# A second first-stage table, reads back in 4 KB pieces, and staging tiles in other buffers

## The chip, the core and the metric

The kernel runs on one core of one Trainium2 chip. The metric is device time in microseconds (us) of one execution. Before the change the median of 3 runs is 520.27 us (519.3 to 520.41).

## What is computed

Two blocks stand behind each other. The first filters each of 8 sequences (2496 tokens, 256 channels) in the frequency domain; the second sends every token to one of 8 experts, of which each keeps the 80 tokens with the largest gate, and all other rows of the output are zero.

```python
X = np.fft.rfft(x, axis=1); Y = X * (filt_r + 1j * filt_i)[None]
y = np.fft.irfft(Y, n=2496, axis=1).reshape(8 * 2496, 256)
logits = y @ w_gate; expert_idx = np.argmax(logits, axis=1)
gate_w = softmax(logits)[arange(N), expert_idx]
for e in range(8):
    tok = the (at most capacity = 80) tokens of expert e with the largest gate_w
    out[tok] = gate_w[tok, None] * (np.maximum(y[tok] @ w1[e], 0) @ w2[e])
```

## The kernel before, in words

All matmuls are in float32. The transform of 2496 = 39 x 64 points is done in two stages. For every batch b (0 to 7), the first stage (`stage1`, 11 parts k, each of two groups i of three columns) multiplies an x chunk, 117 partitions of 3 x 39 rows, with the table `wf_t` (117 x 120: NJ = 3 columns, 2 for real and imaginary, NS = 20 frequencies). It does that in one of two ways.

- `still` (L331 to L336), for batches 0, 3, 4, 5 and 7: x is the stationary side, in two halves of 128 channels, and `wf_t` moves, through a rearranged view: the table lies as (a s), with a = (real or imaginary, column), and is read as (s a), 20 elements apart. The result lies channel by channel, is copied to `t1` by ScalarE (L377, VectorE for part of batch 0), and `transpose1` (L420, L422) turns it with identity matmuls into `t2` tiles.
- `moving` (L338 to L341), for the batches in `BOUNCE` = (1, 2, 6): `wf_t` is the stationary side and x moves, 256 columns. ScalarE copies the result to a staging tile `sg` (L347, L348, from `t2pool`, 4 tiles that the `t2` of `transpose1` share), stores it to DRAM (L352, 1 KB pieces), and `take` (L407 to L413) reads it back transposed from DRAM: three DMAs for a batch, of partitions 0-48, 48-96 and 96-128, each a row of 20 KB per partition. There are no transposes for these batches.

The second stage (`stage2`, 10 steps u for a batch, so v = 10 b + u from 0 to 79) multiplies with `d_t` (L432), VectorE multiplies the result with the filter (two L440), POOL adds and subtracts (L447). Two steps later `turn` multiplies with the identity and the gate weights at once (L460); ScalarE copies the spectrum out (L476) to `ys` (batches 0 and 1) or `ysp` tiles of `fspool` (3 tiles of 4 KB a partition), which go to DRAM (L453). Logits, gates and each batch's candidates follow from there. After the 80 steps come the choice of the kept tokens, their inverse transform from the spectra read back (L588, L609) and the experts (L1278, L1293).

The order is written out by hand (`manual_schedule`): in step v come stage2(v), `take`, the x loads that are due (`put_x`, with a table `held` of the earliest steps), the transposes of step v + 2, the stage1 parts that `s1_at` lists for v, some zero stores of the output (L202), then turn(v - 2). SP's queue carries, in program order, the x loads, the `d_t` loads, the zero stores and the reads back; ScalarE's queue carries the stores; POOL's the filter loads (L285) and other gathers. The PSUM pool `fps` has 3 banks, which L333, L339, L420 and L432 use in turn. A one-element copy `mark` on POOL (L954) holds the later filter loads until an x chunk has come.

Of the kernel before, what the change touches and what calls it, by code (L numbers as in the profile page):

```python
# [13 lines left out]
F32 = mybir.dt.float32  # L14
BF16 = mybir.dt.bfloat16
I32 = mybir.dt.int32
# [7 lines left out]
B, S, C = 8, 2496, 256  # L24
N = B * S
N1, N2 = 39, 64
NS, NQ = 20, 64
NU = NS // 2

NJ, NG = 3, 21  # L30
# [3 lines left out]
SG = 4  # L34
NP, NA = B // 2, N1 + 1
SP = 32
E, FF = 8, 1024
# [4 lines left out]
def dft_tables():  # L42
    n1, n2 = np.arange(N1), np.arange(N2)
    s, q = np.arange(NS), np.arange(NQ)
    ph = 2 * np.pi * (np.outer(n1, s) % N1) / N1
    w = np.stack([np.cos(ph), -np.sin(ph)], 1)
    wf = np.zeros((N1, NJ, 2, NJ, NS))
    for j in range(NJ):
        wf[:, j, :, j] = w

    k = np.array([[next(m for m in range(i, S, N1) if m % NQ == j) for j in q] for i in s])
    th = 2 * np.pi * (n2[:, None, None] * k % S) / S
    c, sn = np.cos(th), np.sin(th)
    d = np.zeros((2, N2, NS, 2, NQ))
    d[0, :, :, 0], d[1, :, :, 0] = c, sn
    d[0, :, :, 1], d[1, :, :, 1] = -sn, c

    two = np.where(s == 0, 1.0, 2.0) / S
    be = 2 * np.pi * (np.outer(q, n2) % NQ) / NQ
    back = np.zeros((2, NQ, 2, N2))  # L60
    back[0, :, 0], back[1, :, 0] = np.cos(be), -np.sin(be)
    back[0, :, 1], back[1, :, 1] = np.sin(be), np.cos(be)
    wi = np.zeros((4, SP, 2, N1, 4))
    for e in range(4):
        wi[e, :NS, 0, :, e] = (two * np.cos(ph)).T
        wi[e, :NS, 1, :, e] = (-two * np.sin(ph)).T

    n = (39 * n2[:, None] + 64 * n1) % S
    al = 2 * np.pi * (n.reshape(S, 1, 1) * k % S) / S
    rows = np.stack([np.cos(al), -np.sin(al)], 2) * two[:, None, None]  # L70

    frow = np.minimum(k, S - k).reshape(NU, 128).T
    fsig = np.where(k > S // 2, -1.0, 1.0).reshape(NU, 128).T
    f32 = np.float32

    def places(a):
        g = a[:, :NJ * NG].reshape(2, NJ, NG, NS, -1).transpose(2, 0, 1, 3, 4)
        return np.concatenate([g.reshape(NJ * 2 * NG, NS, -1), a[:, -1].reshape(2, NS, -1)])

    return (wf.reshape(NJ * N1, -1).astype(f32), wi.reshape(4 * SP, 2, 4 * N1).astype(f32),  # L80
            places(d).reshape(128, NS, 128).astype(f32), back.reshape(128, 128).astype(f32),
            rows.reshape(S, NS * 128).astype(f32),
            np.ascontiguousarray(frow).astype(np.int32), np.ascontiguousarray(fsig).astype(f32))
# [3 lines left out]
def kernel(  # L87
# [11 lines left out]
    nc = tc.nc  # L99
# [17 lines left out]
    dpool = ctx.enter_context(tc.tile_pool(name="dram", bufs=1, space=DRAM))  # L117

    cand = consts.tile([128, B, KC], F32, name="cand")
    warm = cand[:].rearrange("p b k -> p (b k)").bitcast(BF16)  # L120
    nc.vector.memset(warm, 0.0)
    ident = consts.tile([128, 128], F32, name="ident")
# [33 lines left out]
    for b in range(B):  # L156
# [9 lines left out]
    nc.vector.tensor_scalar(out=thot[:], in0=iota[:, 0:16], scalar1=trow[:, 0:1], scalar2=None,  # L166
                            op0=AL.is_equal)
    ehot_t = consts.tile([E, 128], F32, name="ehot_t")
    ecol_i = consts.tile([128, 128], I32, name="ecol_i")
    nc.vector.tensor_single_scalar(out=ecol_i[:], in_=iota_i[:], scalar=E - 1,  # L170
                                   op=AL.bitwise_and)
    ecol = consts.tile([128, 128], F32, name="ecol")
    nc.vector.tensor_copy(out=ecol[:], in_=ecol_i[:])
    nc.vector.tensor_scalar(out=ehot_t[:], in0=ecol[0:E], scalar1=pid[0:E, 0:1], scalar2=None,
                            op0=AL.is_equal)
    same = consts.tile([128, 128], BF16, name="same")
    nc.vector.tensor_scalar(out=same[:], in0=ecol[:], scalar1=lane[:, 0:1], scalar2=None,
                            op0=AL.is_equal)
    before = consts.tile([128, 128], BF16, name="before")
    nc.vector.tensor_scalar(out=before[:], in0=iota[:], scalar1=pid[:, 0:1], scalar2=None,  # L180
# [60 lines left out]

    zs = [consts.tile([128, 2, E, SP], F32, name=f"z_{i}") for i in range(2)]
    key = consts.tile([128, 48, E], F32, name="key")
    kt = consts.tile([128, 2, N2, 4], F32, name="kt")

    with ExitStack() as actx:
        bctx = ExitStack()
# [18 lines left out]

        NM = NJ * 2 * NS
        t_dram, takes = {}, []
        wf_t = tpool.tile([NJ * N1, NM], F32, name="wf_t")
        d_t = tpool.tile([128, NS, 128], F32, name="d_t")  # L270
        e_t = lpool.tile([128, 2 * N2], F32, name="e_t")
# [53 lines left out]
        def stage1(b, k):  # L325
            xt = st["x", b, 2 * k // JC]
            full = 2 if k < NB - 1 else 1
            nk = 2 if full == 2 or b % NJ == 0 else 1
            trio = [i for i in range(B) if min(i - i % NJ, B - NJ) == min(b, B - NJ)]

            def still(ps, i):  # L331
                for cb in range(NDB):
                    nc.tensor.matmul(  # L333
                        out=ps[:, i, NM * cb:NM * cb + NM],
                        lhsT=xt[0:NJ * N1, (2 * k + i) % JC, 128 * cb:128 * cb + 128],
                        rhs=wf_t[:].rearrange("p (a s) -> p s a", s=NS), start=True, stop=True)  # L336

            def moving(ps, i):  # L338
                nc.tensor.matmul(  # L339
                    out=ps[0:NM, i], lhsT=wf_t[:],  # L340
                    rhs=xt[0:NJ * N1, (2 * k + i) % JC, :], start=True, stop=True)  # L341

            if b in BOUNCE:
                ps = fps.tile([128, 2, C], F32, name=f"pa_{b}_{k}", tag="f")
                for i in range(nk):
                    moving(ps, i)
                sg = t2pool.tile([128, 2, C], F32, name=f"sg_{b}_{k}", tag="t2")  # L347
                nc.scalar.copy(out=sg[0:NM, 0:nk], in_=ps[0:NM, 0:nk])  # L348
                if k == 0:
                    t_dram[b] = dpool.tile([128, NS, C], F32, name=f"t_{b}")  # L350
                p0 = 2 * NJ * 2 * k
                nc.scalar.dma_start(  # L352
                    out=t_dram[b][p0:p0 + 2 * NJ * full].rearrange("(i a) s c -> (a s) i c", i=full),
                    in_=sg[0:NM, 0:full])
                if nk > full and b % NJ == 0:
                    left = [i for i in trio if i not in BOUNCE]
                    put_last(b, sg[:, 1])
                    if left:
                        assert len([i for i in trio if i in BOUNCE]) == 1
                        ps = fps.tile([128, 2, NDB * NM], F32, name=f"pm_{b}", tag="f")  # L360
                        still(ps, 1)
                        keep_left(left[0], ps[:, 1], 128)
                elif k == NB - 1:
                    put_last(b, st["left"])
                if k in (3, 7, NB - 1):
                    takes.append((b, k))
                return

            if k == 0:
                st["t1", b] = t1pool.tile([128, NDB * NS, 128], F32, name=f"t1_{b}", tag="t1")  # L370
            t1 = st["t1", b]
            ps = fps.tile([128, 2, NDB * NM], F32, name=f"pa_{b}_{k}", tag="f")
            for i in range(nk):
                still(ps, i)
            copy = nc.vector.tensor_copy if b == 0 and k % 3 == 1 else nc.scalar.copy
            p0 = 2 * NJ * 2 * k
            copy(out=t1[:, :, p0:p0 + 2 * NJ * full].rearrange("p a (i g) -> p a i g", i=full),  # L377
                 in_=ps[:, 0:full].rearrange("p i (a g) -> p a i g", a=NDB * NS))

            def last(src, copy):  # L380
                copy(out=t1[:, :, 128 - 2:128],
                     in_=src.rearrange("p (a r j) -> p j a r", r=2, j=NJ)[:, place3(b)])

            if k == 0 and b % NJ:
                last(st["left"][:, 0:NDB * NM], nc.gpsimd.tensor_copy)
            elif nk > full:
                last(ps[:, 1], nc.scalar.copy)
                if any(i in BOUNCE for i in trio):
                    pm = fps.tile([128, 2, C], F32, name=f"pm_{b}", tag="f")
                    moving(pm, 1)  # L390
                    keep_left(b, pm[0:NM, 1], NM)
                else:
                    keep_left(b, ps[:, 1], 128)
# [13 lines left out]
        def take(v):  # L407
            while takes and v >= NU * (takes[0][0] - 1):
                b, k = takes.pop(0)
                p0, p1 = {3: (0, 48), 7: (48, 96), NB - 1: (96, 128)}[k]  # L410
                if k == 3:
                    st["t1", b] = t1pool.tile([128, NS, C], F32, name=f"t1_{b}", tag="t1")
                nc.sync.dma_start(out=st["t1", b][p0:p1], in_=t_dram[b][p0:p1])  # L413

        def transpose1(b, u):
            t1 = st["t1", b]
# [481 lines left out]
        with tc.manual_schedule():  # L898
# [49 lines left out]
            load_filter(0, 1)  # L948
            for t in (lg, zero_t, *zs, key, kt):
                nc.gpsimd.memset(t[:], 0.0)  # L950
            nc.gpsimd.tensor_copy(out=gi[:, 0, 0:128], in_=ident[:])
            nc.gpsimd.tensor_copy(out=gi[:, 1, 0:128], in_=ident[:])
            mark = tpool.tile([1, 1], F32, name="mark")
# [754 lines left out]
```

## Time and profile before

| | |
|---|---|
| median of 3 runs | 520.27 us |
| the profiled execution, in all | 521.89 us |
| its span | 520.1 us |
| its mean granted TensorE clock | 0.967 |
| DMA, whole span | 125.06 MB in 48852 packets, 240 GB/s |
| queue of SP (q1), of ScalarE (q10), of POOL (q0) | 50.4%, 15.7%, 6.9% of 16 engines |

The profile gives for each engine the time in which it was busy; TensorE has two rows, PE for the matmuls and PEld for the loads of the stationary side, which overlap. A float32 matmul stands there as two instructions. A group line names the source line, the engine, the tiles, the shapes and the count; then busy time, mean length of one, and the idle time before them with what ended it. Matmuls are pipelined, so the length of one is longer than its turn; the turn is read from the starts in the timeline. "A <- B" in a list of waits means that A's engine was idle until B was done; the numbers are the total in us, the times, the longest.

### The profile page before, as it was taken

How to read it: one execution, taken by the hardware profiler on the slowest of the kernel's cores; microseconds unless marked ns; L12 is line 12 of the kernel's file. 1: busy time of each engine (PE TensorE's matmuls, PEld its weight loads, DVE VectorE, ACT ScalarE, POOL GpSimd, SP SyncE). 2: the span in 40 equal slices, each digit the busy share in tenths (PEclk: the TensorE clock that was granted, in tenths of full speed). 3: DMA queues.
4: the chain of work that ended last, by engine and by line, in shares of the span. 5: the costliest groups of instructions: out<-in, count | busy, mean ns of one | idle time of the engine just before them, and what ended most of it. 6: DMA issues, size and time to landing. Idle time of an engine off the chain costs nothing. (4 is left out here: it accounts for less than half of the span.)

```text
span 520.1 us, 8285 instructions
## 1 busy us (share of the span) xinstructions
PE 474.5 (91%) x3127; PEld 434.6 (84%) x3127; DVE 192.6 (37%) x580; ACT 169.1 (33%) x331; POOL 178.9 (34%) x247
## 2 busy tenths in 40 slices
PE   8999478798999999999849999999998999999993
PEld 6978368697999999999739999988887888898882
DVE  2154134262455244345414527894772000001100
ACT  1245123232234444445414234543322223111110
POOL 7458214342243334324213434553226600221211
PEclk8999789898999999999979999999999999999998
DMA  7549677898777757767878996328979799199800
GB/s 213 174 136 251 178 219 217 213 268 286 236 231 260 243 203 230 283 212 227 247 191 280 331 373 262 163 83 311 375 277 361 264 365 355 46 372 371 277 16 18
DMA packets 48852, 125.06 MB, mean 240 GB/s; under 512 B 6035, under 2 KB 24537, under 8 KB 47651
## 3 DMA queue, kind: packets, MB, share of 16 engines
q1 hardware_dynamic: 29606, 83.67, 50.4%
q10 hardware_dynamic: 14701, 28.92, 15.7%
q0 software_dynamic: 4496, 11.85, 6.9%
q8 instruction: 27, 0.44, 0.3%
q14 instruction: 22, 0.18, 0.1%
HBM read 76.23 MB, written 51.07 MB: 245 GB/s over the span
## 5 line engine op out<-in xcount | busy, mean ns | idle before, releaser
L447 POOL TENSOR_TENSOR p<-p,p 128x256 f32<-128x256 f32 x154 | 109.6, 733 | 204.9 <-DVE p L440 144.6
L440 DVE TENSOR_TENSOR p<-pb,ft 128x512 f32<-128x512 f32 x160 | 102.2, 680 | 16.2 <-PE pb L432 16.1
L333 PE MATMUL pa<-wf_t,x 117*128 117x120 f32 x428 | 101.1, 397 | 1.8 <-DMA x<-in_x_dram 1.4
L460 PE MATMUL py<-gi,p 128*128 128x136 f32 x640 | 90.8, 286 | 1.3 <-POOL p L447 0.7
L460 PEld LDWEIGHTS py<-gi,p 128*128 128x128 f32 x640 | 88.0, 197 | 4.1 <-POOL p L447 1.1
L333 PEld LDWEIGHTS pa<-wf_t,x 117*128 117x128 f32 x428 | 84.5, 209 | 7.3 <-DMA x<-in_x_dram 1.9
L432 PE MATMUL pb<-d_t,t 128*128 128x128 f32 x640 | 86.8, 279 | 3.8 <-DMA t<-t 2.3
L432 PEld LDWEIGHTS pb<-d_t,t 128*128 128x128 f32 x640 | 79.8, 195 | 5.2 <-issue 2.4
L483 DVE COPY z<-py 128x16 f32<-128x16 f32 x60 | 11.1, 186 | 136.1 <-ACT ysp L476 92.0
L609 PE MATMUL po<-yb,wt 128*128 128x256 f32 x240 | 56.9, 381 | 2.0 <-ACT wt L602 1.5
L377 ACT COPY t<-pa 128x480 f32<-128x480 f32 (+1 forms) x51 | 27.7, 543 | 84.0 <-PE pa L333 77.8
L609 PEld LDWEIGHTS po<-yb,wt 128*128 128x128 f32 x240 | 43.4, 190 | 7.3 <-ACT wt L602 1.8
L339 PE MATMUL pa<-x,wf_t 117*120 117x256 f32 x128 | 37.0, 423 | 13.5 <-ACT t L422 7.3
L422 ACT COPY t<-pt 128x512 f32<-128x512 f32 x50 | 29.1, 584 | 43.8 <-PE pt L420 30.7
L476 ACT COPY ysp<-py 128x512 f32<-128x512 f32 x60 | 35.3, 588 | 19.1 <-PE py L460 15.3
L339 PEld LDWEIGHTS pa<-x,wf_t 117*120 117x120 f32 x128 | 23.8, 204 | 19.1 <-ACT t L422 8.3
L420 PE MATMUL pt<-ident,t 128*128 128x128 f32 x200 | 30.5, 276 | 9.4 <-ACT sg L348 8.8
L602 ACT COPY wt<-pw 128x512 f32<-128x512 f32 x39 | 22.7, 586 | 49.9 <-PE pw L597 41.3
L348 ACT COPY sg<-pa 120x512 f32<-120x512 f32 (+1 forms) x33 | 18.9, 573 | 42.4 <-PE pa L339 24.8
L420 PEld LDWEIGHTS pt<-ident,t 128*128 128x128 f32 x200 | 23.6, 142 | 9.9 <-ACT sg L348 9.2
L1278 PEld LDWEIGHTS ph<-xs,w 128*128 128x128 f32 x256 | 29.6, 192 | 0.6
L1278 PE MATMUL ph<-xs,w 128*128 128x80 f32 x256 | 29.5, 274 | 0.0
(215 smaller groups left out, 390.8 us busy)
## 6 DMA issues: line engine op xcount, KB each, us to landing
out_dram<-zero_t SPq DMA_DIRECT2D x64, 312.0 KB
x<-in_x_dram SPq DMA_DIRECT2D x40, 468.0 KB
w<-in_moe_w_dram SPq DMA_DIRECT2D x16, 1024.0 KB
yf<-ysp ACTq DMA_DIRECT2D x30, 512.0 KB
yb<-yf SPq DMA_DIRECT2D x6, 2560.0 KB
t<-sg ACTq DMA_DIRECT2D x30, 240.0 KB
t<-t SPq DMA_DIRECT2D x6, 960.0 KB
yf<-ys ACTq DMA_DIRECT2D x10, 512.0 KB
```

The lines of the kernel that those rows point to most:

```text
L333: nc.tensor.matmul(out=ps[:, i, NM * cb:NM * cb + NM], lhsT=xt[0:NJ * N1, (2 * k + i) % JC, 128 * cb:128 * cb + 128], rhs=wf_t[:].rearrang ...
L339: nc.tensor.matmul(out=ps[0:NM, i], lhsT=wf_t[:], rhs=xt[0:NJ * N1, (2 * k + i) % JC, :], start=True, stop=True)
L377: copy(out=t1[:, :, p0:p0 + 2 * NJ * full].rearrange("p a (i g) -> p a i g", i=full), in_=ps[:, 0:full].rearrange("p i (a g) -> p a i g", ...
L420: nc.tensor.transpose(ps[:, i, cb, :], t1[:, NS * cb + 2 * u + i, :], ident[:])
L422: nc.scalar.copy(out=t2[:].rearrange("p i c -> p (i c)"), in_=ps[:].rearrange("p i c q -> p (i c q)"))
L432: nc.tensor.matmul(out=ps[:, cb, i], rhs=d_t[:, 2 * u + i, :], start=True, stop=True, lhsT=t2[:, i, 128 * cb:128 * cb + 128])
L440: nc.vector.tensor_tensor(out=pt, in0=ps[:].rearrange("p c s r q -> p (c s) r q"), in1=f.unsqueeze(2).to_broadcast([128, 2 * NDB, 2, NQ]), ...
L447: adder.tensor_tensor(out=yt[:, :, r, :], in0=yt[:, :, r, :], in1=pr[1][:, :, 1 - r, :], op=op)
L460: nc.tensor.matmul(out=ps[:, i, ZW * cb:ZW * cb + ZW], rhs=gi[:, cb, :], lhsT=yt[:, 2 * cb + i].rearrange("p r q -> p (r q)"), start=True, ...
L476: nc.scalar.copy(out=dst.rearrange("p s (h w) -> p s h w", h=2), in_=pv[:, :, :, 0:128])
L609: nc.tensor.matmul(pos[t][:, 0, 0:C], lhsT=wts[t, g // 2][:, g % 2, i, :], rhs=ybs[t][:, s, :], start=(s == 0), stop=(s == NS - 1))
L1278: nc.tensor.matmul(ph[:, fc // 4, fc % 4, 0:cap], lhsT=self.w1s[e][:, k, 128 * fc:128 * fc + 128], rhs=xs[:, k, :], start=(k == 0), stop=( ...
```

## The change

The host table is laid out as (s a), so `still` reads it as it lies. A second tile `wm_t` gets the order (a s) from one POOL copy, and `moving` takes it. The reads back get a limit of 4096 bytes for a piece (the DMA's shape becomes 48 x 5 x 1024 in place of 48 x 5120). The staging tiles of batches 1 and 2 come from `fspool` (the 3 tiles that `ysp` uses later); batch 6's stay in `t2pool`. Two constant tiles, `ecol_i` and `ecol`, become views of `kt`, which is allocated earlier; POOL clears `kt` in the start phase, as before, now after VectorE's last read of `ecol`. On each engine the order of the instructions stays, but for the added copy on POOL between the clearing of `kt` and the first copy of `gi`.

```diff
-    wf = np.zeros((N1, NJ, 2, NJ, NS))
+    wf = np.zeros((N1, NJ, NS, 2, NJ))
     for j in range(NJ):
-        wf[:, j, :, j] = w
+        wf[:, j, :, :, j] = w.transpose(0, 2, 1)
...
+    kt = consts.tile([128, 2, N2, 4], F32, name="kt")
...
-    ecol_i = consts.tile([128, 128], I32, name="ecol_i")
+    ecol_i = kt[:, 0].rearrange("p n c -> p (n c)")[:, 0:128].bitcast(I32)
...
-    ecol = consts.tile([128, 128], F32, name="ecol")
+    ecol = kt[:, 1].rearrange("p n c -> p (n c)")[:, 0:128]
...
+        wm_t = tpool.tile([NJ * N1, NM], F32, name="wm_t")
         wf_t = tpool.tile([NJ * N1, NM], F32, name="wf_t")
...
-                        rhs=wf_t[:].rearrange("p (a s) -> p s a", s=NS), start=True, stop=True)
+                        rhs=wf_t[:], start=True, stop=True)
...
-                    out=ps[0:NM, i], lhsT=wf_t[:],
+                    out=ps[0:NM, i], lhsT=wm_t[:],
...
-                sg = t2pool.tile([128, 2, C], F32, name=f"sg_{b}_{k}", tag="t2")
+                if b < NY + 1:
+                    sg = fspool.tile([128, SG, C], F32, name=f"sg_{b}_{k}", tag="fs")
+                else:
+                    sg = t2pool.tile([128, 2, C], F32, name=f"sg_{b}_{k}", tag="t2")
...
-                nc.sync.dma_start(out=st["t1", b][p0:p1], in_=t_dram[b][p0:p1])
+                nc.sync.dma_start(out=st["t1", b][p0:p1], in_=t_dram[b][p0:p1],
+                                  max_dma_last_dim=4096)
...
+            nc.gpsimd.tensor_copy(out=wm_t[:].rearrange("p (a s) -> p a s", s=NS),
+                                  in_=wf_t[:].rearrange("p (s a) -> p a s", s=NS))
             nc.gpsimd.tensor_copy(out=gi[:, 0, 0:128], in_=ident[:])
```

More of the change, by code (lines that the diff above doesn't have):

```diff
@@ L168 @@
     ehot_t = consts.tile([E, 128], F32, name="ehot_t")
-    ecol_i = consts.tile([128, 128], I32, name="ecol_i")
-    nc.vector.tensor_single_scalar(out=ecol_i[:], in_=iota_i[:], scalar=E - 1,
+    ecol_i = kt[:, 0].rearrange("p n c -> p (n c)")[:, 0:128].bitcast(I32)
+    nc.vector.tensor_single_scalar(out=ecol_i, in_=iota_i[:], scalar=E - 1,
                                    op=AL.bitwise_and)
-    ecol = consts.tile([128, 128], F32, name="ecol")
-    nc.vector.tensor_copy(out=ecol[:], in_=ecol_i[:])
-    nc.vector.tensor_scalar(out=ehot_t[:], in0=ecol[0:E], scalar1=pid[0:E, 0:1], scalar2=None,
+    ecol = kt[:, 1].rearrange("p n c -> p (n c)")[:, 0:128]
+    nc.vector.tensor_copy(out=ecol, in_=ecol_i)
+    nc.vector.tensor_scalar(out=ehot_t[:], in0=ecol[0:E, :], scalar1=pid[0:E, 0:1], scalar2=None,
                             op0=AL.is_equal)
     same = consts.tile([128, 128], BF16, name="same")
-    nc.vector.tensor_scalar(out=same[:], in0=ecol[:], scalar1=lane[:, 0:1], scalar2=None,
+    nc.vector.tensor_scalar(out=same[:], in0=ecol, scalar1=lane[:, 0:1], scalar2=None,
                             op0=AL.is_equal)
@@ L243 @@
     key = consts.tile([128, 48, E], F32, name="key")
-    kt = consts.tile([128, 2, N2, 4], F32, name="kt")
     with ExitStack() as actx:
```

## The prediction

> **What bounds the kernel now.** I read, in this order, the busy shares of the page, its costliest groups, a table of windows by stage, the timeline of TensorE inside a stage, and the list of waits. The page's chain of work is of no use here: it holds only the last 3 us. The page first:
>
> ```profile
> PE 474.5 (91%) x3127; PEld 434.6 (84%) x3127; DVE 192.6 (37%) x580; ACT 169.1 (33%) x331; POOL 178.9 (34%) x247
> ...
> L333 PE MATMUL pa<-wf_t,x 117*128 117x120 f32 x428 | 101.1, 397 | 1.8 <-DMA x<-in_x_dram 1.4
> L460 PE MATMUL py<-gi,p 128*128 128x136 f32 x640 | 90.8, 286 | 1.3 <-POOL p L447 0.7
> ...
> L432 PE MATMUL pb<-d_t,t 128*128 128x128 f32 x640 | 86.8, 279 | 3.8 <-DMA t<-t 2.3
> ```
>
> TensorE is the only engine near full. L333 has a third fewer instructions than L460 or L432, each narrower (120 columns against 136 and 128), yet is the costliest: 101.1/428 = 236 ns of busy time each against 142 and 136. The windows (PE, PEld, DVE, ACT, POOL busy, clock, DMA share, GB/s) say where TensorE is full:
>
> ```profile
> 6.00:26.00 20.00, 19.94 (x90) 18.86 (x91) 4.93 (x28) 4.71 (x9) 11.08 (x17) 0.91 0.70 207
> 26.00:54.00 28.00, 25.89 (x185) 22.55 (x183) 14.48 (x36) 12.72 (x25) 19.11 (x24) 1.00 0.75 188
> 54.00:121.00 67.00, 48.22 (x300) 44.34 (x301) 23.81 (x73) 19.85 (x36) 19.77 (x29) 0.87 0.80 221
> 121.00:239.00 118.00, 118.00 (x803) 114.45 (x802) 51.29 (x135) 47.35 (x87) 39.09 (x57) 0.99 0.74 244
> 239.00:287.00 48.00, 38.13 (x268) 34.94 (x268) 19.43 (x52) 19.36 (x35) 14.66 (x22) 0.93 0.84 236
> 287.00:327.00 40.00, 40.00 (x272) 38.69 (x273) 20.58 (x50) 14.32 (x32) 16.49 (x24) 1.00 0.84 315
> ```
>
> So 6-26 (first stage of batch 0), 121-239 (batches 3 to 5) and 287-327 (batch 7) are TensorE's; 54-121 (batches 1 and 2, which go through DRAM) and 239-287 (batch 6, likewise) wait, with the clock down after each wait. From 327 on nothing is touched. One full step of the middle stage:
>
> ```profile
> 148.46 1.92 PE L333 MATMUL pa<-wf_t,x 117*128 117x120 f32 x8
> 150.20 1.11 PE L460 MATMUL py<-gi,p 128*128 128x136 f32 x8
> 151.15 1.05 PE L432 MATMUL pb<-d_t,t 128*128 128x128 f32 x8
> 152.04 1.92 PE L333 MATMUL pa<-wf_t,x 117*128 117x120 f32 x8
> ```
>
> The step takes 3.58 us. A step that has only L432 and L460 (the timeline from 108.44 to 110.26) takes 1.82. Eight L333 therefore cost 1.76 us, 220 ns each, twice what L432 (0.89 us for eight) takes for more columns. Wait lines of 28-125:
>
> ```profile
> ACT sg L348 <- DMA t<-sg: 14.1, 3, 9.9
> ...
> PE pt L420 <- ACT sg L348: 7.6, 1, 7.6
> ...
> PE pa L339 <- DMA x<-in_x_dram: 4.9, 2, 3.8
> ACT t L422 <- DMA t<-sg: 4.8, 2, 3.5
> ...
> PE pf L302 <- ACT t L422: 3.8, 1, 3.8
> ...
> PE pb L432 <- DMA t<-t: 2.3, 1, 2.3
> ```
>
> A staging tile can't be refilled before its store has landed; ACT, in order, holds everything behind it, and TensorE runs out of PSUM.
>
> **The change part by part.** *The table.* L333 reads its moving side with 80 bytes between elements; L339 reads 256 contiguous columns at 0.86 us per four, 215 ns, its full rate. With (s a) order L333 reads contiguously. Its operands, loads and counts are else those of L432, so I take 0.89 us for eight (bound by the 128-column load) and a saving of 0.87 us per eight, 109 ns each. The bounds of that saving are 0 (the stride is not the cause) and 126 ns (if 120 columns ran at L339's per-column rate, 101 ns less a little load); L432 is nearest. L339 keeps a contiguous table as weights.
>
> - 6-26: 88 instructions at 224 ns, 19.7 us. At 109 ns they would need 9.8, but now x comes late. By the packet records of the trace the five 468 KB chunks end at 5.0, 6.8, 9.0, 12.0 and 14.3 us, and a waiter starts some 1.1 us after (4.99 to 6.06). The last of the 4 KB chunks is thus usable at 15.5, then two parts of 0.9 and the last one: the end is at about 18.4 instead of 25.6. Saving 7.2, not 10. The filter loads behind the POOL mark (13.4) are in by 22, before the loop asks for them.
> - 121-239 (with the first eight at 115): 256 instructions, 27.9 us. Something comes late next: three PSUM banks serve L333, L420 and L432 in turn, and VectorE's two L440 products (1.28 us) free a bank about 1.7 us after L432 ends. With two fast parts and a transpose between, the bank is asked for after 0.44+0.87 = 1.3 us; seven such steps at 0.4, and a dozen steps with gating on VectorE at 0.2, give back 5. Saving 23.
> - 287-327: 84 instructions, 9.2 us, 2 back likewise. Saving 7.
> - The 4 L333 in batch 6's stage lie among waits: nothing.
>
> *The second table itself*: one POOL copy of 117x120; the 128x128 copy L951 took 0.30 us, so 0.3 to 0.6 us. It lies before the mark, which waits for x until 13.37 while POOL has been idle for 1.87. *Its neighbours*: POOL's clearing of kt now waits for VectorE's last read of ecol (L177, 16.0 now). That is queued behind the L377 copy of part 4, which itself comes with the faster matmuls at about 11; POOL is then free at about 13, with gi, the mark and the six filter loads queued behind. I count 0; if the cover fails, up to 2 us on loads that have 3 to spare. Two fewer 128x128 tiles cost no time.
>
> *The reads in pieces.* The packet records show each 20 KB row as one packet. The first-third reads (48 rows) last 48.2-55.7, 90.5-97.5 and 256.4-264.8, mean 2.08 us a packet; rows of the later reads to all 128 partitions take 0.77 to 0.90. Meanwhile the other queue starves: no 1 KB store packet starts from 47.6 to 54.5. By the 4 KB packets of x (159 ns uncontended) fifteen pieces per engine would take 2.4 us instead of 7.5, the x chunk behind them in SP's queue would come 5 us sooner in three places, and 54-287 would gain 15 us more. [...] What they change is turn-taking: at 91-96 the records show one 1 KB packet per 20 KB packet and engine; with 4 KB pieces (about 0.45 us each) fifteen store packets need some 8 us beside a first third, and the read may be 1 us longer for them. Bounds per read: 3 us better, 3 us worse. DMA issue on SP rises from 0.33 to at most x's 0.85 us.
>
> *Staging tiles in the stores' buffers.* Batch 1's stores get a ring of three of their own; batch 0's transposes keep four tiles and no longer wait for stores. For batch 2, which had all four tiles alone, three is one fewer. Their first later user (ysp, at 135 now) comes long after.
>
> Waits of 26-121, at their cost now with the cold clock after:
> - 7.6 at 54-61.6 and 1.5 cold. The tile is free after the change, but the part after next needs an x chunk that stands behind the 7.5 us read: it ended at 58.3, TensorE used it at 62.5. About 5 stay. Gain 4.
> - 3.8 at 69-72.9, 1.4 cold, 1.35 at 81.3: the transpose's wait goes; late next is the last read of batch 1 (part 10's copy to its first use took 9.9 us, with 7.2 of warm work beside): 3.3 stay. Gain 3.3.
> - small waits at 36-51: 0.8.
> - 3.8 at 96.7 for x behind batch 2's first read: stays, 1 worse for the shared read and the smaller ring.
> - 2.3 at 118 with 0.9 cold: its store stood behind a read (blocked to 112); gain 2.
>
> Together 9. Of 239-287 only the pieces act (batch 6 keeps its tiles): the 7.0 us wait at 263-270 is for a store blocked from 257 to 262 by the read; some 3.5 go.
>
> **Sum.** 7.2 + 9 + 23 + 3.5 + 7 = 49.7 us from the profiled execution's 521.9 (its span is 520.1): 472.2. The median of the runs shown is 1.6 lower, so 471.
>
> **The rivals.** (1) *The transfers don't yield*: stores still starve, or the ring of three binds; the 12.5 us of the DRAM stages vanish. For: 75 us of DMA busy time lie at 30-120, more than TensorE's work there. 483 to 490. (2) *The middle stage becomes another's*: 87 us of DMA time must pass in 95 us, and yf's stores, VectorE at 2.5 us of 2.7 in gating steps, or the PSUM banks hold it. Against: SP's x loads wait 74.5 us for TensorE to free buffers, so they run ahead. Half of the 30 is lost: 486. (3) *It goes better*: pieces also unblock x; 450 to 458. (4) *The table does not do what it says*: L333 stays at 220 ns since the cause is not the stride; only the 12.5 remain: 508. Speaks against: all else of it equals L432. (5) *Slower*: pieces lose their turn against other queues. 120 pieces per engine in nine reads must outweigh the table's 37 us, 0.31 us more each; at 0.35, 42 us, it is 526. Against: the longest 4 KB packet in the trace took 0.59 us where a piece's share of 20 KB is already 0.46.
>
> **How the numbers follow.** Main case 0.58 (its own range 463 to 479), rival 1 0.20, 2 0.10, 3 0.07, 4 0.03, 5 0.02. The range takes the main case, most of 1 and 2 and the upper edge of 3: 457 to 491. About 0.2% is what a measurement of this kernel can tell from no change: faster 0.97, same 0.01, slower 0.02.
>
> **What would show it.** Right: L333 near 110 ns a piece (busy about 50 us for 428), TensorE's idle moved to 8-18 with x as releaser, the middle stage near 95 us, no POOL delay of filter loads, L348's waits for t<-sg much shorter. [...]

## The result and the profile after

The changed kernel takes 481.82 us (median of 4 runs, 477.99 to 483.09) against 520.34 of the kernel before on the same chip (519.30 to 521.21): a ratio of 0.925, 95% interval 0.919 to 0.931. The profiled execution took 483.09 us with a span of 481.2 and a granted clock of 0.961. For that execution the prediction's sum was 472.2, so 10.9 us of the gain did not come. Five executions in the groups below (488.46 to 496.06 us) are over 1.5% above the fastest of their kernel; the ratios and their intervals leave these out, the medians do not. In the lines of the changed kernel L334 is the old L333, L340 the old L339, L352 the copy to `sg`, L437 the old L432, L465 the old L460.

The page, busy shares and two groups:

```profile
PE 431.4 (90%) x3127; PEld 396.8 (82%) x3127; DVE 191.9 (40%) x580; ACT 169.0 (35%) x331; POOL 179.8 (37%) x248
...
L437 PE MATMUL pb<-d_t,t 128*128 128x128 f32 x640 | 87.2, 280 | 10.2 <-DMA t<-t 5.9
...
L334 PE MATMUL pa<-wf_t,x 117*128 117x120 f32 x428 | 58.5, 287 | 3.2 <-DMA x<-in_x_dram 2.0
L340 PE MATMUL pa<-x,wm_t 117*120 117x256 f32 x128 | 37.7, 430 | 23.5 <-DMA x<-in_x_dram 14.9
```

The group of L334 fell from 101.1 to 58.5 us; an instruction is now as long as one of L437. The idle time went elsewhere: L437 waits 10.2 us where it was 3.8, and L340 has 23.5 us of idle time before it where it was 13.5. The windows, cut at the same events of the program as before (PE, PEld, DVE, ACT, POOL busy, clock, DMA share, GB/s; the share adds up the durations of packets over 16 engines, so it can come out a little over 1):

```profile
6.00:20.00 14.00, 13.02 (x92) 12.58 (x93) 4.91 (x28) 4.72 (x9) 9.16 (x16) 1.00 0.89 260
20.00:54.00 34.00, 25.43 (x188) 22.66 (x186) 15.92 (x40) 14.72 (x28) 22.84 (x29) 0.96 0.83 209
54.00:115.00 61.00, 45.89 (x292) 41.57 (x292) 22.10 (x68) 18.05 (x33) 18.32 (x26) 0.86 0.78 212
115.00:211.00 96.00, 94.24 (x804) 94.08 (x805) 50.70 (x134) 46.70 (x87) 39.34 (x57) 0.96 0.91 303
211.00:260.00 49.00, 38.14 (x272) 34.70 (x271) 20.07 (x54) 19.44 (x36) 15.14 (x22) 0.93 0.83 237
260.00:290.00 30.00, 30.00 (x267) 30.00 (x266) 19.12 (x46) 14.00 (x32) 16.25 (x24) 1.00 1.02 377
```

The three stages of TensorE became shorter: 6-26 is 6-20, the middle stage 118 us is 96, batch 7's 40 is 30. The two DRAM stretches did not. 26-121 was 95 us long with 20.9 of TensorE idle in it; 20-115 is 95 us long with 23.7. 239-287 was 48, 211-260 is 49. The DMA share of the middle went from 0.74 to 0.91, of batch 7's stretch from 0.84 to 1.02. A step of the middle stage, in the timeline of TensorE:

```profile
137.39 1.05 PE L334 MATMUL pa<-wf_t,x 117*128 117x120 f32 x8
138.28 1.10 PE L465 MATMUL py<-gi,p 128*128 128x136 f32 x8
139.21 1.05 PE L437 MATMUL pb<-d_t,t 128*128 128x128 f32 x8
140.10 1.05 PE L334 MATMUL pa<-wf_t,x 117*128 117x120 f32 x8
```

2.71 us from L334 to L334, where it was 3.58; its own turn is 0.89 us, where it was 1.76 (137.39 to 138.28). The waits of 28-125:

```profile
PE pa L340 <- DMA x<-in_x_dram: 14.9, 4, 8.5
...
ACT sg L352 <- DMA t<-sg: 7.9, 2, 6.8
PE pb L437 <- DMA t<-t: 5.9, 1, 5.9
PE pb L437 <- issue: 4.0, 1, 4.0
```

The transpose's 7.6 us for a staging tile are gone, and so is more than half of ScalarE's waits for stores (7.9 us, where it was 14.1 before the copies to `sg` and 4.8 before those of the transposes). The longest, 6.8, is now in batch 2, which has the ring of three: the three `fspool` tiles, used in turn. In their place TensorE waits for x, 14.9 us where it was 4.9, and for the reads back, 9.9 where it was 2.3. The stretch of batch 1 shows it in order of time:

```profile
46.52 0.60 PE L425 MATMUL pt<-ident,t 128*128 128x128 f32 x4
55.66 3.74 PE L340 MATMUL pa<-x,wm_t 117*120 117x256 f32 x8 [8.53 <-DMA x<-in_x_dram]
...
62.96 0.60 PE L340 MATMUL pa<-x,wm_t 117*120 117x256 f32 x2
...
70.24 1.09 PE L465 MATMUL py<-gi,p 128*128 128x136 f32 x8
75.34 2.05 PE L437 MATMUL pb<-d_t,t 128*128 128x128 f32 x8 [4.01 <-issue]
```

Part 8 of batch 1 waited 8.53 us for the x chunk behind the first-third read; before, it was the transpose ahead of it that waited, 7.58. Part 10 starts at 62.96; its result must be stored and read back before the second stage of batch 1 can start at 75.34, and TensorE has 8.4 us of work until it stops at 71.33 (part 10 included). The read was issued at 69.26, so I take the 4.01 us that the profile puts down to "issue" for this read too.

Events of both kernels, from the timelines (us):

| | before | after | gain in between | predicted |
|---|---|---|---|---|
| L339/L340 of batch 0 (end of its first stage) | 25.60 | 19.37 | 6.2 | 7.2 |
| part 8 of batch 1 | 62.48 | 55.66 | 0.6 | 4 (+0.8) |
| second stage of batch 1 | 82.63 | 75.34 | 0.5 | 3.3 |
| part 8 of batch 2 | 100.45 | 95.31 | -2.2 | -1 |
| second stage of batch 2 | 120.14 | 116.58 | -1.6 | 2 |
| part 0 of batch 6 | 240.62 | 212.75 | 24.3 | 23 |
| part 0 of batch 7 | 286.90 | 259.67 | -0.6 | 3.5 |
| L649/L654, end of what the change touches | 326.94 | 290.62 | 9.1 | 7 |
| end of the span | 520.09 | 481.23 | 2.5 | 0 |

### The profile page after: what moved, and what is told of

The parts are those of the page before. It is cut to its first block, busy times and chain, and to the rows that moved or that the text cites. A ratio compares the mean times of both kernels' runs of the same rounds, so it can differ in the third digit from the quotient of the medians.

```text
span 481.2 us, 8289 instructions
## 1 busy us (share of the span) xinstructions
PE 431.4 (90%) x3127; PEld 396.8 (82%) x3127; DVE 191.9 (40%) x580; ACT 169.0 (35%) x331; POOL 179.8 (37%) x248
## 3 DMA queue, kind: packets, MB, share of 16 engines
q1 hardware_dynamic: 31142, 83.67, 54.5%
## 5 line engine op out<-in xcount | busy, mean ns | idle before, releaser
L445 DVE TENSOR_TENSOR p<-pb,ft 128x512 f32<-128x512 f32 x160 | 102.2, 681 | 20.3 <-PE pb L437 20.2
L437 PE MATMUL pb<-d_t,t 128*128 128x128 f32 x640 | 87.2, 280 | 10.2 <-DMA t<-t 5.9
L465 PE MATMUL py<-gi,p 128*128 128x136 f32 x640 | 89.7, 284 | 1.4 <-POOL p L452 0.7
L437 PEld LDWEIGHTS pb<-d_t,t 128*128 128x128 f32 x640 | 79.7, 195 | 11.7 <-issue 10.3
L465 PEld LDWEIGHTS py<-gi,p 128*128 128x128 f32 x640 | 83.4, 195 | 3.2 <-POOL p L452 1.2
L334 PE MATMUL pa<-wf_t,x 117*128 117x120 f32 x428 | 58.5, 287 | 3.2 <-DMA x<-in_x_dram 2.0
L340 PE MATMUL pa<-x,wm_t 117*120 117x256 f32 x128 | 37.7, 430 | 23.5 <-DMA x<-in_x_dram 14.9
L334 PEld LDWEIGHTS pa<-wf_t,x 117*128 117x128 f32 x428 | 54.8, 203 | 4.7 <-DMA x<-in_x_dram 2.0
L488 DVE COPY z<-py 128x16 f32<-128x16 f32 x60 | 11.2, 187 | 97.8 <-ACT ysp L481 65.6
L340 PEld LDWEIGHTS pa<-x,wm_t 117*120 117x120 f32 x128 | 24.0, 206 | 29.6 <-issue 14.9
L352 ACT COPY sg<-pa 120x512 f32<-120x512 f32 (+1 forms) x33 | 18.9, 574 | 46.2 <-PE pa L340 34.7
L1285 PEld LDWEIGHTS ph<-xs,w 128*128 128x128 f32 x256 | 29.6, 192 | 0.6
L1285 PE MATMUL ph<-xs,w 128*128 128x80 f32 x256 | 29.5, 274 | 0.0
L1300 PE MATMUL po<-w,hT 128*80 128x256 f32 x128 | 28.8, 379 | 0.0
```

The lines of the kernel that those rows point to most:

```text
L334: nc.tensor.matmul(out=ps[:, i, NM * cb:NM * cb + NM], lhsT=xt[0:NJ * N1, (2 * k + i) % JC, 128 * cb:128 * cb + 128], rhs=wf_t[:], start=T ...
L340: nc.tensor.matmul(out=ps[0:NM, i], lhsT=wm_t[:], rhs=xt[0:NJ * N1, (2 * k + i) % JC, :], start=True, stop=True)
L437: nc.tensor.matmul(out=ps[:, cb, i], rhs=d_t[:, 2 * u + i, :], start=True, stop=True, lhsT=t2[:, i, 128 * cb:128 * cb + 128])
L445: nc.vector.tensor_tensor(out=pt, in0=ps[:].rearrange("p c s r q -> p (c s) r q"), in1=f.unsqueeze(2).to_broadcast([128, 2 * NDB, 2, NQ]), ...
L465: nc.tensor.matmul(out=ps[:, i, ZW * cb:ZW * cb + ZW], rhs=gi[:, cb, :], lhsT=yt[:, 2 * cb + i].rearrange("p r q -> p (r q)"), start=True, ...
L1285: nc.tensor.matmul(ph[:, fc // 4, fc % 4, 0:cap], lhsT=self.w1s[e][:, k, 128 * fc:128 * fc + 128], rhs=xs[:, k, :], start=(k == 0), stop=( ...
```

## The experiments

Each group below had its own runs of the kernel before beside it; kernels of different groups are compared by their ratios to that. A ratio stands with its 95% interval, which is 2 to 4 us wide to each side.

Theory 1, after seeing the result: the table gave the whole gain. The other two parts gave nothing because the first-third reads are held by where their rows land, whatever their pieces; x and stores stand behind them. Theory 2: the pieces hurt by themselves, and hide a gain of the staging. Theory 3: the ring of three hurts in batch 2. Theory 4 came up after the second group: the end of a batch's transform is set by a chain (last part, store, read back) that no wait ahead of it governs.

### The parts of the change, alone and left out

Table only:

```diff
-                if b < NY + 1:
-                    sg = fspool.tile([128, SG, C], F32, name=f"sg_{b}_{k}", tag="fs")
-                else:
-                    sg = t2pool.tile([128, 2, C], F32, name=f"sg_{b}_{k}", tag="t2")
+                sg = t2pool.tile([128, 2, C], F32, name=f"sg_{b}_{k}", tag="t2")
...
-                nc.sync.dma_start(out=st["t1", b][p0:p1], in_=t_dram[b][p0:p1],
-                                  max_dma_last_dim=4096)
+                nc.sync.dma_start(out=st["t1", b][p0:p1], in_=t_dram[b][p0:p1])
```

> Only the second table; reads in 20 KB rows and staging tiles as before. Theory 1 (the table gave all of the 38.5 us, the other two parts give nothing net because the first-third reads are held by where their rows land): 479 to 485, the middle stage 27 to 28 us shorter than before, the 7.6 us transpose wait for a staging tile at about 48 still there, so batch 1's second stage begins no more than 1 to 2 us later than in the changed kernel. As the prediction had it (staging and pieces worth 9 + 3.5 in the DRAM stages): 491 to 495. Theory 2 (the pieces hurt): 474 to 479. Theory 3 (the ring of three hurts): 474 to 479 as well; the next two runs part them.

Only the second hunk of it (table and staging, whole rows):

> The changed kernel with its reads back in whole 20 KB rows (no pieces). Theory 1: within 2 us of the changed kernel's 481.8; the first-third reads take 7 to 8.5 us as with pieces. Theory 2 (pieces shut the 1 KB stores out and lengthen the reads): 3 to 8 us faster, 1 KB store packets pass again at about one for each 20 KB packet and engine, and the ring wait of 6.8 us in batch 2 shrinks. As the prediction had it (pieces let stores take turns): 3 to 6 us slower.

Only the first hunk of it (table and pieces):

> The changed kernel with the staging tiles back in the four that batch 0's transposes share. Theory 1: within 2 us of 481.8, since behind the staging wait stands the x chunk that the first-third read delays. Theory 3 (three tiles bind in batch 2): 3 to 8 us faster, batch 2's second stage begins earlier and batch 1's no later. As the prediction had it (7.6 + 3.8 us of waits go by the separate ring): 5 to 8 us slower.

The kernel before, with the limit of 4096 bytes on the reads as its only change:

> The kernel before with only the reads back cut into pieces of 4 KB. Theory 1: 517 to 523, no difference beyond the noise, first-third reads again 7 to 8.5 us long. Theory 2 (pieces hurt by themselves): 524 to 530, with no 1 KB store packet during the first thirds. As the prediction had it: 3 to 8 us faster.

| kernel | median us | before, same chip | ratio (95%) |
|---|---|---|---|
| table only | 484.81 | 522.36 | 0.930 (0.923 to 0.936) |
| table and staging | 484.34 | 522.36 | 0.930 (0.925 to 0.935) |
| table and pieces | 485.43 | 522.36 | 0.927 (0.922 to 0.933) |
| pieces only | 523.46 | 522.36 | 1.003 (0.9995 to 1.007) |

The table alone gives all of the gain that can be told from the noise: the intervals of the three kernels with the table overlap each other's and the changed kernel's, and that of the pieces alone takes in no change. A gain or loss of 2 or 3 us from the other two parts would not show. Table only, the same stretch of TensorE's timeline:

```profile
48.22 1.05 PE L433 MATMUL pb<-d_t,t 128*128 128x128 f32 x8
56.68 1.11 PE L421 MATMUL pt<-ident,t 128*128 128x128 f32 x4 [7.41 <-ACT sg L349]
57.59 3.62 PE L340 MATMUL pa<-x,wm_t 117*120 117x256 f32 x8
```

With the old staging tiles the 7.41 us wait for a tile is back, and part 8 starts at 57.59 instead of 55.66. So the 8.53 us of waiting for x took the place of the 7.41 for the tile. It is not a full exchange: the second stage of batch 1 begins at 79.26, 3.9 us later than in the changed kernel (75.34), where theory 1 had 1 to 2. The times bear out theory 1 where it says what gave the gain, not yet its reason. Theory 2 (pieces hurt) and theory 3 (the ring hurts) would each have made one of these kernels 3 to 8 us faster than the changed kernel, and none is, by the ratios. As for the turns of the stores, the packet records count how many 1 KB store packets start while the 48 rows of a first third are under way (batches 1, 2, 6):

| | read lasts, us | store packets in it |
|---|---|---|
| before | 7.5, 7.0, 8.4 | 27, 115, 101 |
| table only | 7.4, 6.8, 8.0 | 28, 77, 114 |
| table and staging | 7.0, 7.1, 7.4 | 108, 126, 115 |
| changed kernel | 7.2, 6.8, 6.8 | 12, 86, 78 |
| changed kernel, second profile | 7.7, 7.6, 7.0 | 104, 196, 83 |

For the changed kernel the read is taken as the first 240 packets of 4 KB in SP's queue after its issue. The x chunk behind it has packets of the same size, and with whole rows, where the two can be told apart, 7 to 75 of the x packets start before the last row is in; so the lengths with pieces are the least that they can be, and it is not shown that pieces shorten the read. Nor is it shown that they change the turns: the counts of two profiles of the changed kernel differ as much (12 and 104, 86 and 196) as those of different kernels. Only batch 6 agrees with itself: 73 to 87 in the six profiles with pieces that keep the rows and the queue order, 101 to 115 in the three with whole rows, so no more pass there with pieces. The prediction counted on 240 in a read (fifteen on each of 16 engines).

The separate staging tiles do leave a mark. From the first packet of batch 1's first third to the last of the x chunk behind it, the four kernels in which batches 0 and 1 share their tiles took 9.9 to 10.3 us, with 163 to 185 store packets in that time. The five profiles with tiles of their own, and rows and queue order unchanged, took 11.1 to 12.4 us, with 203 to 267. Stores that are no longer held up run beside the read and the chunk for which TensorE then waits.

### Where the rows land, and the order in the queue

A part has 12 rows, and which rows it has is free, as long as `d_t` has the same order. The rows of each third on both sides of 60, in two reads:

```diff
+POS = [12 * i for i in (0, 1, 5, 6, 2, 3, 7, 8, 4, 9, 10)]
...
-                p0, p1 = {3: (0, 48), 7: (48, 96), NB - 1: (96, 128)}[k]
+                parts = {3: ((0, 24), (60, 84)), 7: ((24, 48), (84, 108)),
+                         NB - 1: ((48, 60), (108, 128))}[k]
...
```

> The changed kernel with the rows of the transform's table permuted, so that each of the three reads of a batch goes to two partition ranges, one below and one above 60 (0-24 with 60-84, 24-48 with 84-108, 48-60 with 108-128; the second stage's rows are permuted alike, the result is the same function). Bytes, pieces and order of the queue stay; each read is two DMAs instead of one. Theory 1 (the first third is held by where its rows land): the 48 rows land in 3 to 4.5 us instead of 7.5 to 8.5, the x waits of 8.5 and 4.4 us at 47 and about 90 shrink to under 4 together, ratio to before 0.905 to 0.912 (471 to 475). Rival (the number of rows and queues per transfer, or DRAM itself, is what holds the read): still 7 to 8 us, ratio within 0.5% of the changed kernel's 0.925.

The same with whole rows:

> As the run before, with whole 20 KB rows instead of 4 KB pieces. Theory 1: the two differ by under 1%; the rows take 0.9 to 1.3 us each instead of 2.08. [...] If pieces only cost issue and turns: 1 to 4 us faster.

x loads ahead of the read back, in the changed kernel:

```diff
+                    put_x(v)
                     take(v)
-                    put_x(v)
```

> The changed kernel with the x loads of a step put into SP's queue ahead of its read back instead of behind it. Theory 1 (TensorE waits for the x chunk that stands behind the first-third read): the x waits of 8.5 and 4.4 us in the stretch 28-125 are gone or under 2 us each, the reads come later by 1 to 2 us; ratio 0.912 to 0.920 (474 to 479). Rival (what holds TensorE is not the order in the queue but the DMA engines as a whole, 0.8 busy there): waits of the same sum under another name (t<-t or t<-sg), ratio 0.921 to 0.930.

| kernel | median us | before, same chip | ratio (95%) |
|---|---|---|---|
| two reads a third, pieces | 491.34 | 522.74 | 0.941 (0.937 to 0.944) |
| two reads a third, rows | 491.60 | 522.74 | 0.939 (0.934 to 0.944) |
| x first | 487.75 | 522.74 | 0.934 (0.930 to 0.939) |

All three are misses for theory 1 as I had it, and the two with two reads a third are slower than the changed kernel. What TensorE waits for in 28-125 tells why; with two reads a third:

```profile
PE pb L444 <- DMA t<-t: 14.8, 2, 8.1
PE pa L345 <- DMA x<-in_x_dram: 7.8, 2, 6.5
```

With x first:

```profile
PE pb L437 <- DMA t<-t: 11.0, 2, 6.0
PE pb L437 <- ACT sg L352: 4.4, 1, 4.4
PE pa L340 <- ACT sg L352: 4.1, 1, 4.1
PE pa L340 <- DMA x<-in_x_dram: 1.2, 1, 1.2
```

The x wait went from 14.9 to 7.8 and to 1.2 us, as theory 1 said. Its time came back under other names: with x first, the ring of three (4.4 and 4.1) and the last read of the batch (11.0, against 5.9 + 4.0); with two reads a third, the last read (14.8). With two reads a third, the end of the chain was slower itself. In batch 1 the store of part 10, issued at 64.01, had landed only at 72.5 (SP's second issue of the last read), where the changed kernel has 64.05 and 69.3. In batch 6 the rows of the last read were in 9.1 us after its second issue (257.8 to 267.0), where in the changed kernel it was 5.6 us (257.5 to 263.1). Its 12 and 20 rows are followed in SP's queue by zero stores, and the packet records show these from 259 on while rows of the read still ran at 266. Whether this is what made it long was not tried alone.

### The first third in the middle, and all waits at once

The changed kernel without an edit, for comparison:

> The changed kernel itself once more, on the same chip as the next runs, to be compared with them: its first result was a ratio to before of 0.925, the seven variants of it so far lie between 0.927 and 0.941. Expected 0.922 to 0.932; its own spread tells what a difference of these kernels has to be to mean something.

The first third in the partitions 36 to 84, in one read as before:

```diff
+POS = [12 * i for i in (3, 4, 5, 6, 0, 1, 2, 7, 8, 9, 10)]
...
-                p0, p1 = {3: (0, 48), 7: (48, 96), NB - 1: (96, 128)}[k]
+                parts = {3: ((36, 84),), 7: ((0, 36), (84, 96)), NB - 1: ((96, 128),)}[k]
...
```

> The changed kernel with the first third of the transform in partitions 36-84 (one read of 48 rows, as many as before, 28 rows below and 20 above 64), the second in 0-36 and 84-96, the last in 96-128 as before. In the run with two reads a third, the first third passed beside the stores, but the last one (12 and 20 rows) took 9 us from issue to use instead of 5.5 to 6; here its rows are where they were. Theory 1 (landing place): first-third read 3 to 4.5 us instead of 7.5 to 8.5, the x waits of 8.5 and 4.4 us less than half, the last read as in the changed kernel, 3 to 8 us faster than the changed kernel on this chip. Theory 4 (the end of a batch's transform is set by the chain from its last part over store and read, and each shortened wait comes back there): x waits shrink, t<-t waits grow by as much, within 3 us of the changed kernel.

In addition:

```diff
-                if b < NY + 1:
+                if b == 1 or b == 2 and k % 2:
...
+                    put_x(v)
                     take(v)
-                    put_x(v)
```

> As the run before, with x loads ahead of the read of the same step, and batch 2's staging tiles taken in turn from the ring of three and from the four tiles that batch 0 no longer needs. Theory 1 with the ring (each of the three things that hold part 8 of batches 1 and 2 is taken away at once): part 10 of batch 1 starts at 55 to 58 instead of 63, the second stage of batch 1 at 68 to 71 instead of 75.3, 8 to 13 us faster than the changed kernel on this chip. Theory 4: part 10 comes earlier, but its store and the last read land no earlier, so the t<-t wait is 9 us or more; 0 to 3 us faster.

| kernel | median us | before, same chip | ratio (95%) | first third and the x chunk next to it, batches 1, 2 | first `moving` of batch 1 to that of batch 6 | from there to the last eight L437 |
|---|---|---|---|---|---|---|
| changed kernel again | 486.31 | 521.39 | 0.928 (0.923 to 0.933) | 12.1, 11.2 | 191.5 | 101.9 |
| first third in 36-84 | 484.04 | 521.39 | 0.926 (0.922 to 0.930) | 7.3, 6.3 | 186.2 | 106.8 |
| the same, x first, more tiles | 483.68 | 521.39 | 0.924 (0.918 to 0.930) | 6.5, 6.8 | 188.8 | 100.9 |

The landing place does set the length of the read: in one DMA of the same pieces, the same 48 rows with the x chunk of 117 packets next to them in the queue are in after 6.3 to 7.3 us instead of 11.2 to 12.1. (The two are counted together because their packets have one size. The read alone, where it goes ahead of the chunk, takes at least 4.6 us in 36-84 and at least 6.6 in 0-48.) But the kernel's time does not follow: the three intervals overlap, and what theory 1 hoped for, 8 to 13 us with all waits taken away, is not there.

The second kernel is not as theory 4 had it either. Its waits for `t<-t` did not grow (3.2 us in 28-125), and up to the first `moving` of batch 6 it is 5.3 us ahead (186.2 against 191.5). It loses 4.9 behind that: batch 6's second stage begins 54.5 us after this batch's first `moving`, against 49.7. What lengthens that stretch was not found.

In the last kernel, part 10 of batch 1 starts 8.3 us earlier than in the first profile of the changed kernel, at 54.62, and this is what it gets for it (timeline of TensorE):

```profile
54.62 0.69 PE L345 MATMUL pa<-x,wm_t 117*120 117x256 f32 x2 [1.30 <-ACT sg L357]
...
74.32 2.05 PE L443 MATMUL pb<-d_t,t 128*128 128x128 f32 x8 [9.09 <-DMA t<-t]
```

and its windows:

```profile
44.00:54.00 10.00, 9.32 (x67) 8.16 (x65) 4.20 (x12) 3.90 (x9) 5.75 (x8) 1.00 1.00 289
54.00:64.00 10.00, 7.82 (x46) 7.18 (x47) 4.54 (x14) 4.46 (x9) 2.81 (x4) 0.83 0.89 227
64.00:74.00 10.00, 1.23 (x10) 1.00 (x8) 1.24 (x5) 1.17 (x2) 1.40 (x2) 0.80 0.90 249
```

The second stage of batch 1 starts at 74.32, against 75.34 in the changed kernel and 76.48 in the kernel with the first third in the middle alone. Part 10's store is issued at 57.12; SP, free since 63.96, can issue the last read only at 67.89, when that store and the two left-over rows stored right behind it (`left`, to which the profile puts the wait) have landed; the rows are first used at 74.32. DMA is 0.9 to 1.0 busy all the while (44 to 74) and TensorE is busy 1.23 us of the last ten. That is what theory 4 said: the end of a batch's transform hangs on the chain from its last part over store and read. The events of batch 1 in eight profiles, in us from its first `moving`:

| kernel | part 10 | its store is issued | SP is free for the last read | last read issued | second stage |
|---|---|---|---|---|---|
| before | 40.4 | 45.1 | 42.4 | 48.8 | 54.6 |
| table only | 42.1 | 47.1 | 44.1 | 51.3 | 57.5 |
| changed kernel, two profiles | 41.2, 40.6 | 42.3, 41.7 | 43.2, 42.5 | 47.5, 47.7 | 53.6, 54.6 |
| two reads a third, pieces | 42.0 | 43.1 | 44.6 | 51.6 | 57.9 |
| x first | 35.2 | 37.7 | 44.1 | 45.2 | 52.4 |
| first third in 36-84 | 36.1 | 37.2 | 41.7 | 45.5 | 51.4 |
| the same, x first, more tiles | 32.1 | 34.6 | 41.5 | 45.4 | 51.8 |

Part 10 comes up to 9 us earlier, the last read only some 2. Two things hold the read, and no run parts them. The stores behind part 10 take longer: from the store's issue to the read's, 10.8 us in the last kernel against 5.2 and 6.0, with the DMA engines 0.89 busy from 54 to 64 and 0.90 from 64 to 74 (in the changed kernel 0.72 from 64 to 69.3). And SP, which works in order, is not free before 41.5 in any of them, mostly because an x load of batch 2 ahead of the read waits for VectorE (5.0 us in the first profile of the changed kernel); with x first that is nearly all of it, since SP waits only about 1 us more for the stores. No version here is shown to beat the changed kernel.

### How far apart columns may lie

Every element twice, so 8 bytes apart:

```diff
-    return (wf.reshape(NJ * N1, -1).astype(f32), wi.reshape(4 * SP, 2, 4 * N1).astype(f32),
+    return (np.repeat(wf.reshape(NJ * N1, -1), 2, 1).astype(f32), wi.reshape(4 * SP, 2, 4 * N1).astype(f32),
...
-        wf_t = tpool.tile([NJ * N1, NM], F32, name="wf_t")
+        wf_w = tpool.tile([NJ * N1, NM, 2], F32, name="wf_t")
+        wf_t = wf_w[:, :, 0]
...
```

> The changed kernel with the table stored with every element twice, so that the matmuls with x as the stationary side read it 8 bytes apart instead of 4 (80 apart before the change). If any step over 4 bytes halves the moving side: eight of them cost 1.76 us again and the time is about 519. [...]

Stored in four interleaved runs, so 16 bytes apart:

```diff
+    wf = wf.reshape(NJ * N1, 4, -1).transpose(0, 2, 1)
...
-                        rhs=wf_t[:], start=True, stop=True)
+                        rhs=wf_t[:].rearrange("p (c d) -> p d c", d=4), start=True, stop=True)
...
```

> The changed kernel with the table stored so that the matmuls with x as the stationary side read it 16 bytes apart, in four runs of 30 elements, and the second table made from it by four small copies. At 8 bytes a step eight of them took 0.89 us as with contiguous columns. [...] If the cost begins at a wider step: 0.89 and about 482. If it grows with the step: between, 1.0 to 1.5.

8 bytes apart (one run, 482.82 us):

```profile
138.72 1.05 PE L335 MATMUL pa<-wf_t,x 117*128 117x120 f32 x8
139.62 1.09 PE L466 MATMUL py<-gi,p 128*128 128x136 f32 x8
```

16 bytes apart (one run, 521.51 us, beside 521.39 for before):

```profile
143.64 1.90 PE L335 MATMUL pa<-wf_t,x 117*128 117x120 f32 x8
145.36 1.11 PE L466 MATMUL py<-gi,p 128*128 128x136 f32 x8
```

0.90 us for eight against 1.72: contiguous (0.89) and 8 bytes apart go at one rate, 16 and 80 bytes apart (1.72 and 1.76) at about half of it; 12 bytes was not tried, and what halves the rate was not shown. At 16 bytes the whole gain of the change is gone, with its staging and its pieces in place. Rival 4 of the prediction (the cause is not the stride) is excluded by this.

## Why the prediction was right, and where it was off

The time lies in the range, above the main case's own 463 to 479, just under rival 1 (483 to 490, "the transfers don't yield"), which is what happened in the DRAM stages. The table's part of the prediction was right in mechanism and size. The 12.5 us of the other two parts (9 and 3.5) were wrong: measured, they are a loss of 3.3. It is in part luck that the median is only 10.8 above the forecast of 471: three terms that were too small gave back 5.9.

- *L333's turn*: predicted 0.89 us for eight, measured 0.89. That 120 columns take as long as L437's 128 agrees with the bound that the prediction took, the 128-column load; so does L1285 of the experts, whose 80 columns behind such a load take 0.89 us for eight as well (64 in 7.10 us from 423.31). No run varied the load. The middle stage gave 24.3 us for 23. Of the 27.9 that 256 instructions could save, 5 were to be lost to PSUM banks; 3.6 were lost, and mostly not to them. TensorE waited 0.2 us for VectorE's L445 in 115-211. But the stage now begins behind a wait of 5.9 us instead of 2.3, with a granted clock of 0.50 from 115 to 120 (0.66 from 119 to 124 before), and its first three groups (L437, sixteen L334, L465) take 3.1 us more than their warm turns add up to, where it was 0.9. Batch 7's stretch gave 9.1 for 7: the 2 taken off did not come either.
- *Start of stage 1*: 6.2 for 7.2, with 2.0 us of waiting for x, as predicted. But this run was a good one. Counted to the first `moving` of batch 1, ten profiles with the fast table (all but that of two reads a third in rows) lie between 20.9 and 25.2 us (mean 23.2), three with the slow one between 27.9 and 28.4 (mean 28.1): 4.9 on average. In the second run of the changed kernel, L340 comes as early (19.34), and the loss starts behind it: VectorE's copy of the last part begins at 21.02 instead of 19.57, and TensorE waits for VectorE. What holds that copy was not found. POOL's filter loads begin at 15.62 where they began at 13.70, behind the clearing of `kt` (14.01): the 2 us of "if the cover fails". No wait in the profile of the changed kernel is put down to them.
- *The step that failed*: "What they change is turn-taking: ... with 4 KB pieces (about 0.45 us each) fifteen store packets need some 8 us beside a first third". In the two profiles of the changed kernel 12 and 104, 86 and 196, 78 and 83 store packets passed in the three reads; none had the fifteen an engine (240 in all) that were counted on, and batch 6 had fewer than with whole rows (101 to 115). The 3.5 us of batch 6, which stood on this alone, were -0.6: the stretch 211-260 has a wait of 7.3 us where it was 7.0. Pieces alone gave a ratio of 1.003, not clear of no change. Two readings of the packet records in the prediction were off as well: the mean of 2.08 us a packet is that of the first of the three reads (all three: 2.02), and 0.59 us is not the longest 4 KB packet of the trace before, which has some of 1.3 us in 30-125 and of 2.2 in 125-255. The second stood against rival 5, which did not come all the same.
- *The waits of 26-121*: 9 predicted, -2.7 measured. The waits that I struck off did go. Each was costed by what was due next on the same engine, taken at the time at which it came before; yet that, too, hung on transfers, and TensorE reached them sooner. "About 5 stay" at part 8 were 8.5; "3.3 stay" at the second stage of batch 1 were 4.0 plus a cold clock (0.66 granted from 75 to 80); at batch 2, the 2 us gain was a loss of 1.6. What stands in its place is in the table of batch 1's events: whichever wait is taken away, another one comes up before the second stage. From the table alone to the changed kernel that event moves from 57.5 to 53.6 and 54.6, 2.9 to 3.9 us of the 8.1 that were counted up to there; at the second stage of batch 3 (129.5 against 128.6 and 129.1) 0.4 to 0.9 are left.
- *The length of a first third*: the prediction let the read keep its length in pieces ("about 5 stay" and "stays, 1 worse" among the waits of 26-121 count on that). That was the author's estimate; no trace of the kernel before shows what pieces do to a read. What its packet records show is the place: 48 whole rows took 7.0 to 8.4 us in 0-48 and 4.7 to 4.8 in 48-96. In the other runs it was 6.8 to 8.0 with whole rows in 0-48, and in pieces at least 6.6 there and at least 4.6 in 36-84. Why the place counts was not shown, and the kernel's time did not follow it (ratios of 0.928 in 0-48 and 0.926 in 36-84, with intervals that overlap).
- *The tail*: 2.5 us less from the end of the loop on, not predicted. From the first L597/L602 behind the loop to the end it is 162.8 us before, 160.2 after, 161.5 in the second run of the changed kernel, 161.9 in the 16-byte kernel; so at least half is scatter. The rest is open.

The sum: the waits of 26-121 fell short by 11.7, batch 6 by 4.1, the start by 1.0; the middle, batch 7 and the tail gave 1.3, 2.1 and 2.5 more. That is the 10.9 us.

## What to carry to other kernels

Look at how the moving operand of each matmul lies: a second copy of a small table, made once, was worth 37 us of 522 here (33 to 40), and the row that told it was a group with fewer and narrower instructions and more time. In a stretch like 20-115 here, with the DMA engines 0.83 busy up to 54 and 0.78 from there, and TensorE waiting for several transfers in turn, do not add up the waits that a change strikes off; follow the chain (last part, store, read, first use) to the event that opens the next stage, and ask whether that one moves. Taking away one, two or three of the waits ahead of it moved that event by a few us at most, and made no kernel measurably faster than the changed one. Compare two profiles of one kernel before reading a count or a wait of a single one.

## What the runs showed of the hardware

- A float32 moving operand of 120 columns took 0.89 and 0.90 us for eight with its elements 4 and 8 bytes apart, and 1.72 and 1.76 with 16 and 80. 12 bytes was not tried.
- Where rows land counted: 48 rows with the x chunk next to them took 11.2 to 12.1 us with the rows in 0-48 and 6.3 to 7.3 with them in 36-84, in kernels run beside each other. Cutting the rows into five pieces counted for nothing that the time shows (with the table and the staging, ratios of 0.930 in rows and 0.925 and 0.928 in pieces; pieces alone 1.003).
